# A fused attention and spectral-mixing kernel: the last 64 tokens laid out by batch halves, one of their two slots moved to ninth place, and 18 repeated matmuls added

## Chip, cores, metric

The kernel runs on one core of a Trainium2 chip. The metric is the device time of one execution in microseconds (us). Three runs of the kernel before gave 425.57, 425.76 and 425.96 us; the median, 425.76 us, is the time before.

## What is computed

Sliding-window causal attention (window 64) over 8 batches, 8 heads, 576 tokens and 64 channels a head; its result, as x of shape [8, 576, 512], goes through a spectral mixing layer with 64 modes.

```python
scores = scale * np.matmul(q, k.transpose(0, 1, 3, 2))      # masked to 0 <= rel < 64, then softmax
x = attn_out.transpose(0, 2, 1, 3).reshape(B, S, H * D)     # [8, 576, 512]
X = np.fft.rfft(x, axis=1)                                  # the first 64 modes are used
Yr = np.einsum('bmd,mde->bme', Xr, w_r) - np.einsum('bmd,mde->bme', Xi, w_i)
Yi = np.einsum('bmd,mde->bme', Xr, w_i) + np.einsum('bmd,mde->bme', Xi, w_r)
y = np.fft.irfft(Y, n=S, axis=1)
u = x + y
return u + np.maximum(u @ w_ch, 0.0)                        # float32, [8, 576, 512]
```

The two weight tensors `w_r` and `w_i` are 64 matrices of 512 x 512 in float32 each; all but the imaginary part of mode 0 are read, 127 matrices of 1 MB.

## The kernel before

**Attention, to about 142 us.** Windows of 512 query columns are worked off in a fixed order; the result is kept in SBUF as `x_sb` in bfloat16. A forward transform of the 64 modes by matmuls fills `XQ`.

**The weight stream, to about 390 us.** GpSimd's queue loads the 127 matrices, cast to bfloat16 on the way, one by one (`load_w`, L138) or two at a time (`load_two`, L144), into a ring of SBUF places. `half(i)` (L610) is the product of matrix i with `XQ`: 16 matmuls with 16 columns into one of two PSUM banks, `psys`. The banks change after 8 modes; at the change the finished one is copied to `YT` or `YTl`. `issue(i)` loads ahead as ring places come free, so a load waits on PE for the matmuls that read the place last. Other work is laid between the halves by a table of steps: from i = 33 the channel product of x (`channel_turn`, `channel`, into `Z0`), in 20 steps (`tables`) the tables of the inverse transform, `trigI` and `trigL`, and then the inverse transform of the first 48 modes (`add_z`, `make_u`, `last_tile`). Where little other work lies between two halves late in the stream, `fill(i)` (L895) repeats a matmul with 512 columns whose result is not used (`idle`, L900, PE row L902).

**The end.** The output has 36 pieces of 128 rows and 512 columns, 256 KB each. They are grouped in 18 slots of two pieces (index j). Slot s < 16 holds rows 128t to 128t + 127 of two batches (p, t = s // 4, s % 4). Slots 16 and 17 hold the last 64 tokens of four batches each: slot 16 of batches 0 to 3, slot 17 of batches 4 to 7. A piece of them is the last tokens of two batches. Before, the rows of such a piece are interleaved: partition 2i + k holds token 512 + i of the pair's batch k. `turns_bf`, a permuted identity, brings x into this order, and the columns of `trigI`, `trigL` and of the copy in `channel_turn` are interleaved in the same way.

The order of the slots is written out by hand: `seq` (L944), where `TURN` marks the place at which the late modes of batches 4 to 7 are turned (`turn_product`, `turn_rows`). For each slot PE lays the finished part of Z into a bank (`lay`, L955) and adds the late modes (`late_rows`, L962); ACT takes the positive part (`rectify`, L980); PE adds the late modes of the second term; DVE adds the kept u (`final`, L985), and SP stores the result. All stores go out on SP's queue in this order. The first two slots and the last one are stored piece by piece (L988), the others by one transfer of 512 KB for both pieces, whose pattern counts 128 partitions outermost (L991). Slots 16 and 17 take two transfers each: `out_of` gives, for each k, every second partition, 64 of them, with both pieces inside.

Of the kernel before, what the change touches and what calls it, by code (L numbers as in the profile page):

```python
# [10 lines left out]
FP32R = mybir.dt.float32r  # L11
# [9 lines left out]
def view(ap, off, dims):  # L21

    return bass.AP(ap.tensor, ap.offset + off, [list(ap.ap[0])] + [list(d) for d in dims])
# [3 lines left out]
def kernel(  # L27
# [17 lines left out]
    NT = 5  # L45
# [35 lines left out]
    def x_rows(b, t, n=128):  # L81
        return x_sb[:n, b // 2, (b % 2) * NT + block(b, t), :]
# [440 lines left out]
    YTl = late.tile([128, NC, B, R], FP32R, name="YTl")  # L523
    wlow = p2.enter_context(tc.tile_pool(name="wlow", bufs=1, side="right", reuse_waits="tile"))
    late2 = p2.enter_context(tc.tile_pool(name="late2", bufs=1, side="right", reuse_waits="tile"))
    trigI = late2.tile([128, S + 66], FP32R, name="trigI")
    trigL = late2.tile([128, S + 64], FP32R, name="trigL")

    py = ExitStack()
    turns_bf = late2.tile([128, 64, 2], BF16, name="turns_bf")  # L530

    ps_y = py.enter_context(tc.tile_pool(name="ps_y", bufs=1, space=PSUM, side="right", reuse_waits="tile"))
    psys = [ps_y.tile([128, DM], FP32, name=f"psy{i}") for i in range(2)]
# [113 lines left out]
    def inverse_tables():  # L647

        c = claim("tables", FP32)
        tmpi = Parts(c[0])  # L650
        pcol = tmpi.tile([128, 1], FP32, name="pcol")
        nc.gpsimd.iota(pcol, pattern=[[0, 1]], base=0, channel_multiplier=1,
                       allow_small_or_imprecise_dtypes=True)

        SW = S // 4
        pos = tmpi.tile([128, SW], FP32, name="pos")
        nc.gpsimd.iota(pos, pattern=[[1, SW]], base=0, channel_multiplier=0,
                       allow_small_or_imprecise_dtypes=True)
        nc.vector.tensor_copy(out=turns_bf, in_=view(ident_bf, 0, [[1, 64], [64, 2]]))

        def col(name):
            return tmpi.tile([128, 1], FP32, name=name)

        def floor(d, p, name):
            f = col(name)
            nc.vector.tensor_scalar(out=f, in0=p, scalar1=1.0 / d, scalar2=0.5 / d - 0.5,
                                    op0=ALU.mult, op1=ALU.add)
            nc.vector.tensor_scalar(out=f, in0=f, scalar1=MAGIC, scalar2=-MAGIC,
                                    op0=ALU.add, op1=ALU.add)
            return f  # L670

        f32 = floor(32, pcol, "f32")
        f64 = floor(64, pcol, "f64")
        lcol, odd, even = col("lcol"), col("odd"), col("even")
        nc.vector.scalar_tensor_tensor(out=lcol, in0=f32, scalar=-32.0, in1=pcol,
                                       op0=ALU.mult, op1=ALU.add)
        nc.vector.tensor_single_scalar(out=lcol, in_=lcol, scalar=float(E0), op=ALU.add)
        nc.vector.scalar_tensor_tensor(out=odd, in0=f64, scalar=-2.0, in1=f32,
                                       op0=ALU.mult, op1=ALU.add)
        nc.vector.tensor_scalar(out=even, in0=odd, scalar1=-1.0, scalar2=1.0,  # L680
                                op0=ALU.mult, op1=ALU.add)
        for tab, row in ((trigI, pcol), (trigL, lcol)):
            yield
            fa, fb = floor(2 * MG, row, "fa"), floor(MG, row, "fb")

            gcol, mcol = col("gcol"), col("mcol")
            nc.vector.scalar_tensor_tensor(out=gcol, in0=fa, scalar=-2.0, in1=fb,
                                           op0=ALU.mult, op1=ALU.add)
            nc.vector.tensor_tensor(out=mcol, in0=fa, in1=fb, op=ALU.subtract)
            nc.vector.scalar_tensor_tensor(out=mcol, in0=mcol, scalar=float(MG), in1=row,  # L690
                                           op0=ALU.mult, op1=ALU.add)
            coef, coefs, coefc = col("coef"), col("coefs"), col("coefc")
            nc.vector.tensor_single_scalar(out=coef, in_=mcol, scalar=0.0, op=ALU.is_equal)
            nc.vector.tensor_scalar(out=coef, in0=coef, scalar1=-1.0 / S, scalar2=2.0 / S,
                                    op0=ALU.mult, op1=ALU.add)
            nc.vector.tensor_tensor(out=coefs, in0=gcol, in1=coef, op=ALU.mult)
            nc.vector.tensor_tensor(out=coefc, in0=coef, in1=coefs, op=ALU.subtract)
            for i in range(4):
                yield
                mt2 = tmpi.tile([128, 2, SW], FP32, name="mti")  # L700
                mt = mt2[:, 0, :]
                nc.vector.tensor_scalar(out=mt, in0=pos, scalar1=float(i * SW), scalar2=mcol,
                                        op0=ALU.add, op1=ALU.mult)
                tis = tmpi.tile([128, SW], FP32, name="tis")
                gen_trig(tmpi, mt2, SW, mt, tis, "i")
                yield
                nc.vector.tensor_scalar(out=tis, in0=tis, scalar1=coefs, scalar2=None, op0=ALU.mult)
                o2 = 513 if tab is trigI else 512
                for c0, c1, o, k in ((0, SW, i * SW, 1),) if i < 3 else ((0, 80, 432, 1), (80, SW, o2, 2)):
                    nc.vector.scalar_tensor_tensor(  # L710
                        out=view(tab, o, [[k, c1 - c0]]), in0=mt[:, c0:c1], scalar=coefc,
                        in1=tis[:, c0:c1], op0=ALU.mult, op1=ALU.add)
        yield
        nc.vector.tensor_scalar(out=view(trigI, 512, [[2, 65]]), in0=trigI[:, 0:65], scalar1=0.0,
                                scalar2=None, op0=ALU.mult)
        last = [view(trigL, 512 + k, [[2, 64]]) for k in range(2)]
        nc.vector.tensor_scalar(out=last[1], in0=last[0], scalar1=odd, scalar2=None, op0=ALU.mult)
        nc.vector.tensor_scalar(out=last[0], in0=last[0], scalar1=even, scalar2=None, op0=ALU.mult)
        give(c)
# [24 lines left out]
    def channel_turn(s):  # L744
        pst = ps_t.tile([128, 2, NC, 128], BF16, name="pxt")
        for j, (b, t) in enumerate(slot_tiles(s)):
            for c in range(NC):
                nc.tensor.transpose(out=pst[:, j, c, :], in_=x_rows(b, t)[:, 128 * c:128 * c + 128],  # L748
                                    identity=ident_bf)
        o, i = xts[s % 2][0], pst.rearrange("p j c n -> p j (c n)")  # L750
        if s >= 4 * NP:
            o, i = (view(a, 0, [[128, 2 * NC]] + d) for a, d in ((o, [[1, 2], [2, 64]]), (i, [[64, 2], [1, 64]])))
        nc.vector.tensor_copy(out=o, in_=i)  # L753

    def channel(s, j):
        if j == 0:
# [37 lines left out]

    def first_rows(ps, b, t, k, x):

        parts = [(b, 128 * t)] if t < NT - 1 else [(b, 513), (b + 1, 512)]
        for n, (bb, o) in enumerate(parts):
            last = n == len(parts) - 1
            nc.tensor.matmul(out=ps, lhsT=trigI[:E0, o:o + 128], rhs=Yp[bb][0][:E0, k, :],  # L800
                             start=n == 0, stop=last and not x)
        if x:
            perm = ident_bf if t < NT - 1 else view(turns_bf, 0, [[1, 128]])
            nc.tensor.matmul(out=ps, lhsT=perm, rhs=x_rows(b, t), start=False, stop=True)

    def add_z(p, t):
        ps = ps_e.tile([128, 2, DM], FP32, name="pse", tag="pse")
# [80 lines left out]
    def out_of(s):  # L888
        if s < 4 * NP:
            p, t = divmod(s, 4)  # L890
            return [(slice(0, 128), out[2 * p:2 * p + 2, 128 * t:128 * t + 128, :])]
        b = 4 * (s - 4 * NP)
        return [(slice(k, 128, 2), out[b + k:b + k + 3:2, 512:576, :]) for k in range(2)]

    def fill(i):  # L895

        if i < T_I - 3 and i in thin:
            idle(psys[1 - mode_of(i) // MG % 2], LEAST - streamed[i])

    def idle(o, n):  # L900
        for _ in range(n):
            nc.tensor.matmul(out=o, lhsT=ident_bf, rhs=view(trigF, 0, [[1, DM]]), start=True, stop=True)  # L902

    with tc.manual_schedule(engines=ALL_FOUR):
# [36 lines left out]


        TURN = -1
        seq = [0, 4, 5, 1, 2, 6, 7, 3, TURN, 8, 12, 9, 13, 10, 16, 17, 14, 11, 15]  # L944
        NQ, TQ = len(seq), seq.index(TURN)
        assert sorted(seq) == list(range(-1, NS))

# [34 lines left out]
        def final(q, js=range(2)):  # L982
            u = U[seq[q]]
            for j in js:
                nc.vector.tensor_tensor(out=u[:, j, :], in0=bank(q, j), in1=u[:, j, :], op=ALU.add)  # L985
                if q in (0, 1, NQ - 1):
                    for pp, o in out_of(seq[q]):
                        nc.sync.dma_start(out=o[j], in_=u[pp, j, :])  # L988
                elif j:
                    for pp, o in out_of(seq[q]):  # L990
                        nc.sync.dma_start(out=o.rearrange("b p e -> p b e"), in_=u[pp])  # L991

        def pool(name, stack=p2, **kw):
            return stack.enter_context(tc.tile_pool(name=name, bufs=1, space=PSUM, reuse_waits="tile", **kw))
# [92 lines left out]
```

## Time and profile before

| What | Value |
|---|---|
| time before, median of 3 | 425.76 us |
| the profiled execution's own time | 425.57 us |
| its span, first to last instruction | 423.8 us |
| mean granted TensorE clock | 0.85 |
| PE matmul busy | 347.9 us, 82% |
| DVE, ACT, POOL busy | 188.8, 159.8, 81.7 us |
| DMA: queue of GpSimd (q0), queue of SP (q1) | 81.21 MB, 10.62 MB |
| HBM read, written | 162.53 MB, 9.44 MB |

Between two numbers divided by a bar, the first is the busy time of a group and the second the mean of one instruction. The span starts at the first instruction; places in it are given in us from there. Shares of busy time are means over the whole span; the stages named above are read one by one.

### The profile page before, as it was taken

To read this page: it belongs to the slowest core of one execution; us is meant where nothing else is said; L and a number is where in the kernel's file an instruction comes from. 1 tells how busy PE (TensorE), PEld (TensorE's weight loads), DVE (VectorE), ACT (ScalarE), POOL (GpSimd) and SP (SyncE) were. 2 spreads that over 40 slices of the span, in tenths; PEclk is the share of its full clock that TensorE was granted. 3 is DMA by queue.
4 is the path that set the end of the run, shared out by engine and by line. 5 is a ranking of instruction groups with operands and counts; after the bars stand their busy time and mean duration, and the time that the engine had idled before them with its cause. 6 is when DMAs were issued, how large, how long until landed. Compare 5 with 4: busy or idle time off the path is not lost.

```text
span 423.8 us, 11431 instructions
## 1 busy us (share of the span) xinstructions
PE 347.9 (82%) x5167; PEld 230.8 (54%) x5167; DVE 188.8 (45%) x359; ACT 159.8 (38%) x267; POOL 81.7 (19%) x146
## 2 busy tenths in 40 slices
PE   7899999999998775957659576667699999898994
PEld 3466666656654575735546455445465565554541
DVE  5576766676764101634341361211104344350885
ACT  5666865766864100212102110200023343330873
POOL 6231222231121230412111111210121112200000
PEclk9999999999999555866665766868579999999997
DMA  8999999999999999999999999999999999995598
GB/s 212 212 214 212 213 214 213 212 213 212 215 213 215 212 216 261 215 213 215 214 213 215 213 216 214 213 215 213 215 214 215 213 213 212 213 214 106 201 381 311
DMA packets 29920, 92.55 MB, mean 218 GB/s; under 512 B 2352, under 2 KB 2352, under 8 KB 29872
## 3 DMA queue, kind: packets, MB, share of 16 engines
q0 software_dynamic: 24624, 81.21, 95.9%
q1 hardware_dynamic: 5248, 10.62, 6.8%
q8 instruction: 40, 0.66, 0.6%
q14 instruction: 8, 0.07, 0.0%
HBM read 162.53 MB, written 9.44 MB: 406 GB/s over the span
## 4 chain that ended last, share of the span: by engine, by line
DMA 41%; PE 39%; DVE 7%; issue 6%; ACT 2%; POOL 0%; DVEq 0%; POOLq 0%; ACTq 0%
DMA wms<-in_moe_w_i_dram 22%; DMA wms<-in_moe_w_r_dram 15%; PE psy L618 6%; PE pso L343 6%; PE pst L247 5%; DMA wls<-in_moe_w_i_dram 5%; PE psv L264 3%; PE psx L365 3%; PE pss L962 2%; DVE x_sb L351 2%; PE pss L300 2%; PE pss L955 2%; PE pss L319 2%; PE psz L759 2%; DVE vT L59 2%
## 5 line engine op out<-in xcount | busy, mean ns | idle before, releaser
L759 PE MATMUL psz<-wch,xT 128*128 128x512 f32 x144 | 63.6, 583 | 0.0
L753 DVE CAST xT<-pxt 128x1024 fp32r<-128x1024 bf16 x18 | 22.0, 1225 | 81.2 <-PE pxt L748 81.0
L762 ACT CAST Z<-psz 128x1024 fp32r<-128x1024 f32 x18 | 18.2, 1012 | 104.2 <-PE psz L759 94.8
L325 ACT ACTIVATE et<-pss 128x512 bf16<-128x512 f32 x72 | 39.2, 600 | 13.7 <-PE pss L319 13.7
L618 PE MATMUL psy<-XQ,wms 128*128 128x16 bf16 x624 | 25.1, 192 | 20.2 <-DMA wms<-in_moe_w_i_dram 14.2
L618 PE MATMUL psy<-XQ,wls 128*128 128x16 bf16 x560 | 21.8, 192 | 23.6 <-DMA wls<-in_moe_w_r_dram 13.7
L759 PEld LDWEIGHTS psz<-wch,xT 128*128 128x128 f32 x144 | 36.6, 281 | 5.9
L618 PEld LDWEIGHTS <-wms 128*128 128x128 bf16 x624 | 21.3, 103 | 32.9 <-DMA wms<-in_moe_w_i_dram 17.6
L618 PEld LDWEIGHTS <-wls 128*128 128x128 bf16 x560 | 19.1, 105 | 33.4 <-DMA wls<-in_moe_w_r_dram 17.1
L343 PE MATMUL pso<-vt,et 128*64 128x65 bf16 (+1 forms) x576 | 32.3, 203 | 3.5 <-DVE x_sb L351 1.8
L811 DVE TENSOR_TENSOR Z<-pse,Z 128x1024 fp32r<-128x1024 f32 x16 | 19.6, 1224 | 29.5 <-PE pse L800 29.5
L343 PEld LDWEIGHTS <-et 128*64 128x64 bf16 (+1 forms) x576 | 22.2, 108 | 14.2 <-issue 6.7
L351 DVE TENSOR_TENSOR x_sb<-pso,rcp 128x640 bf16<-128x640 f32 x32 | 26.3, 822 | 0.9
L618 PE MATMUL psy<-XQ,wt 128*128 128x16 bf16 x560 | 20.5, 192 | 5.5 <-DMA wt<-in_moe_w_i_dram 3.0
L618 PEld LDWEIGHTS <-wt 128*128 128x128 bf16 x560 | 18.4, 104 | 11.3 <-DMA wt<-in_moe_w_i_dram 4.9
L59 DVE COPY vT<-pst 128x768 bf16<-128x768 bf16 x16 | 15.3, 958 | 12.9 <-PE pst L247 11.4
L980 ACT ACTIVATE pss<-pss 128x512 f32<-128x512 f32 x35 | 18.5, 581 | 4.9 <-PE pss L962 4.3
L59 DVE CAST YT<-psy 128x256 fp32r<-128x256 f32 x6 | 2.5, 423 | 38.7 <-PE psy L618 38.7
L748 PE MATMUL pxt<-ident_bf,x_sb 128*128 128x128 bf16 x144 | 15.1, 266 | 2.1 <-issue 2.1
L264 PE MATMUL psv<-ident_bf,vT 128*128 128x128 bf16 (+1 forms) x160 | 15.7, 226 | 0.9 <-DVE vT L59 0.6
L300 PE MATMUL pss<-band,ident_bf 64*64 64x512 bf16 x120 | 16.3, 396 | 0.0
L58 ACT COPY vt<-psv 128x768 bf16<-128x768 bf16 x16 | 12.9, 807 | 8.5 <-PE psv L264 8.4
(191 smaller groups left out, 599.1 us busy)
## 6 DMA issues: line engine op xcount, KB each, us to landing
wt<-in_moe_w_i_dram POOLq DMA_DIRECT2D x19, 512.0 KB, 20.0
wt<-in_moe_w_r_dram POOLq DMA_DIRECT2D x16, 512.0 KB, 19.0
wls<-in_moe_w_r_dram POOLq DMA_DIRECT2D x8, 1024.0 KB, 21.6
wms<-in_moe_w_i_dram POOLq DMA_DIRECT2D x7, 1024.0 KB, 22.0
wms<-in_moe_w_r_dram POOLq DMA_DIRECT2D x7, 1024.0 KB, 21.8
wls<-in_moe_w_i_dram POOLq DMA_DIRECT2D x6, 1024.0 KB, 21.2
rq<-in_q_dram POOLq DMA_DIRECT2D x8, 576.0 KB, 15.3
rv<-in_v_dram POOLq DMA_DIRECT2D x8, 576.0 KB, 13.4
```

The costliest lines, as they stand in the source:

```text
L59: return nc.vector.tensor_copy(out=o, in_=i)
L247: nc.tensor.transpose(out=ps[64 * hh:64 * hh + 64, c, :], in_=src[:, hh, (c0 + c) * D:(c0 + c + 1) * D], identity=ident_bf)
L264: nc.tensor.transpose(out=ps[r0:r0 + n, i, :], in_=vT[:, g, t0:t0 + n], identity=ident_bf)
L300: nc.tensor.matmul(out=pss[(2 * w + hh) % 3][64 * half:64 * half + 64, :], lhsT=ident_bf[pp, pp], rhs=view(band[pp], 128 * half, [[0, WIN ...
L325: nc.scalar.activation(out=et[:, hh, :], in_=pss[(2 * w + hh) % 3], func=ACT_F.Exp, scale=EX_SCALE)
L343: nc.tensor.matmul(out=pso[po, hh, block(b, i // 2) * VW:block(b, i // 2) * VW + D + 1], lhsT=et[pk, hh, col:col + 64], rhs=vt[pk, 1 - f % ...
L351: nc.vector.tensor_tensor(out=view(x_sb, b * NT * DM + g * D, [[4 * D, 2], [DM, NT], [1, D]]), in0=view(pso, 0, [[512, 2], [VW, NT], [1, D]]),
L618: nc.tensor.matmul(out=view(psy, off + 2 * B * e, [[1, 2 * B]]), lhsT=w[:, c, 128 * e:128 * e + 128], rhs=XQ[:, m // HM, c, :, 1 - im:3 - ...
L753: nc.vector.tensor_copy(out=o, in_=i)
L759: nc.tensor.matmul(out=psz[s][:, j, :], lhsT=xts[s % 2][0][:, j, 128 * c:128 * c + 128], rhs=wch[:, c, :], start=(c == 0), stop=(c == NC - 1))
L811: nc.vector.tensor_tensor(out=z, in0=ps, in1=z, op=ALU.add)
L980: nc.scalar.activation(out=bank(q, j), in_=bank(q, j), func=ACT_F.Relu)
```

## The change

- A piece of slots 16 and 17 holds the first of its two batches on partitions 0 to 63 and the second on 64 to 127. `turns_bf` and its copy go, and the strided writes into `trigI`, `trigL` and `xT` become plain ones.
- A piece of slots 16 and 17 is stored as soon as its own add is done, by one transfer from 128 partitions to `out[b:b + 2, 512:576, :]`, instead of two transfers from 64 partitions each after both adds.
- Slot 16 moves from the 15th place to the ninth, ahead of `TURN`; slot 17 moves from the 16th to the 12th place of the slots.
- `fill` adds one repeated matmul after each of the halves 20 to 37.

```diff
-    trigI = late2.tile([128, S + 66], FP32R, name="trigI")
+    trigI = late2.tile([128, S + 128], FP32R, name="trigI")
...
-    turns_bf = late2.tile([128, 64, 2], BF16, name="turns_bf")
...
-        nc.vector.tensor_copy(out=turns_bf, in_=view(ident_bf, 0, [[1, 64], [64, 2]]))
...
-                o2 = 513 if tab is trigI else 512
-                for c0, c1, o, k in ((0, SW, i * SW, 1),) if i < 3 else ((0, 80, 432, 1), (80, SW, o2, 2)):
+                o2 = 576 if tab is trigI else 512
+                for c0, c1, o in ((0, SW, i * SW),) if i < 3 else ((0, 80, 432), (80, SW, o2)):
...
-        nc.vector.tensor_scalar(out=view(trigI, 512, [[2, 65]]), in0=trigI[:, 0:65], scalar1=0.0,
-                                scalar2=None, op0=ALU.mult)
-        last = [view(trigL, 512 + k, [[2, 64]]) for k in range(2)]
+        nc.vector.tensor_scalar(out=view(trigI, 512, [[128, 2], [1, 64]]), in0=view(trigI, 0, [[64, 2], [1, 64]]),
+                                scalar1=0.0, scalar2=None, op0=ALU.mult)
+        last = [trigL[:, 512 + 64 * k:576 + 64 * k] for k in range(2)]
...
-        o, i = xts[s % 2][0], pst.rearrange("p j c n -> p j (c n)")
-        if s >= 4 * NP:
-            o, i = (view(a, 0, [[128, 2 * NC]] + d) for a, d in ((o, [[1, 2], [2, 64]]), (i, [[64, 2], [1, 64]])))
-        nc.vector.tensor_copy(out=o, in_=i)
+        nc.vector.tensor_copy(out=xts[s % 2][0], in_=pst.rearrange("p j c n -> p j (c n)"))
...
-        parts = [(b, 128 * t)] if t < NT - 1 else [(b, 513), (b + 1, 512)]
+        parts = [(b, 128 * t)] if t < NT - 1 else [(b, 576), (b + 1, 512)]
...
-            perm = ident_bf if t < NT - 1 else view(turns_bf, 0, [[1, 128]])
-            nc.tensor.matmul(out=ps, lhsT=perm, rhs=x_rows(b, t), start=False, stop=True)
+            nc.tensor.matmul(out=ps, lhsT=ident_bf, rhs=x_rows(b, t), start=False, stop=True)
...
-            return [(slice(0, 128), out[2 * p:2 * p + 2, 128 * t:128 * t + 128, :])]
+            return out[2 * p:2 * p + 2, 128 * t:128 * t + 128, :]
         b = 4 * (s - 4 * NP)
-        return [(slice(k, 128, 2), out[b + k:b + k + 3:2, 512:576, :]) for k in range(2)]
+        return [out[b + 2 * j:b + 2 * j + 2, 512:576, :] for j in range(2)]
 
     def fill(i):
 
-        if i < T_I - 3 and i in thin:
-            idle(psys[1 - mode_of(i) // MG % 2], LEAST - streamed[i])
+        n = LEAST - streamed[i] if i in thin else i in range(20, 38)
+        if i < T_I - 3:
+            idle(psys[1 - mode_of(i) // MG % 2], n)
...
-        seq = [0, 4, 5, 1, 2, 6, 7, 3, TURN, 8, 12, 9, 13, 10, 16, 17, 14, 11, 15]
+        seq = [0, 4, 5, 1, 2, 6, 7, 3, 16, TURN, 8, 12, 9, 17, 13, 10, 14, 11, 15]
...
-                if q in (0, 1, NQ - 1):
-                    for pp, o in out_of(seq[q]):
-                        nc.sync.dma_start(out=o[j], in_=u[pp, j, :])
+                if q in (0, 1, NQ - 1) or seq[q] >= 4 * NP:
+                    nc.sync.dma_start(out=out_of(seq[q])[j], in_=u[:, j, :])
                 elif j:
-                    for pp, o in out_of(seq[q]):
-                        nc.sync.dma_start(out=o.rearrange("b p e -> p b e"), in_=u[pp])
+                    nc.sync.dma_start(out=out_of(seq[q]).rearrange("b p e -> p b e"), in_=u)
```

More of the change, by code (lines that the diff above doesn't have):

```diff
@@ L707, in inverse_tables @@
                 nc.vector.tensor_scalar(out=tis, in0=tis, scalar1=coefs, scalar2=None, op0=ALU.mult)
-                o2 = 513 if tab is trigI else 512
-                for c0, c1, o, k in ((0, SW, i * SW, 1),) if i < 3 else ((0, 80, 432, 1), (80, SW, o2, 2)):
+                o2 = 576 if tab is trigI else 512
+                for c0, c1, o in ((0, SW, i * SW),) if i < 3 else ((0, 80, 432), (80, SW, o2)):
                     nc.vector.scalar_tensor_tensor(
-                        out=view(tab, o, [[k, c1 - c0]]), in0=mt[:, c0:c1], scalar=coefc,
+                        out=tab[:, o:o + c1 - c0], in0=mt[:, c0:c1], scalar=coefc,
                         in1=tis[:, c0:c1], op0=ALU.mult, op1=ALU.add)
         yield
-        nc.vector.tensor_scalar(out=view(trigI, 512, [[2, 65]]), in0=trigI[:, 0:65], scalar1=0.0,
-                                scalar2=None, op0=ALU.mult)
-        last = [view(trigL, 512 + k, [[2, 64]]) for k in range(2)]
+        nc.vector.tensor_scalar(out=view(trigI, 512, [[128, 2], [1, 64]]), in0=view(trigI, 0, [[64, 2], [1, 64]]),
+                                scalar1=0.0, scalar2=None, op0=ALU.mult)
+        last = [trigL[:, 512 + 64 * k:576 + 64 * k] for k in range(2)]
         nc.vector.tensor_scalar(out=last[1], in0=last[0], scalar1=odd, scalar2=None, op0=ALU.mult)
```

## Prediction

> **What bounds the kernel now.** I read the page's slices and queues first, then the waits, then the end in windows, then the DMA view of the last 12 us.
>
> ```profile
> DMA  8999999999999999999999999999999999995598
> GB/s 212 212 214 212 213 214 213 212 213 212 215 213 215 212 216 261 215 213 215 214 213 215 213 216 214 213 215 213 215 214 215 213 213 212 213 214 106 201 381 311
> DMA packets 29920, 92.55 MB, mean 218 GB/s; under 512 B 2352, under 2 KB 2352, under 8 KB 29872
> ...
> q1 hardware_dynamic: 5248, 10.62, 6.8%
> q8 instruction: 40, 0.66, 0.6%
> ```
>
> The 16 DMA engines are full at some 213 GB/s until 384 us: the weight stream sets the time there. Then a second stage begins, the stores.
>
> ```profile
> POOL wls L144 <- PE psy L618: 70.6, 14, 13.0
> ...
> PEld L618 <- DMA wms<-in_moe_w_i_dram: 17.6, 10, 3.9
> ```
>
> GpSimd waits for PE to free a ring place (total us, times, longest), PE waits for weights; since the engines never run dry, neither costs time.
>
> ```profile
> 400.00:414.00 14.00, 14.00 (x64) 6.71 (x63) 12.79 (x21) 10.03 (x20) 0.00 (x0) 1.00 1.03 381
> 414.00:416.00 2.00, 2.00 (x10) 0.90 (x8) 1.77 (x4) 1.54 (x4) 0.00 (x0) 1.00 0.76 288
> 416.00:422.00 6.00, 1.98 (x7) 0.73 (x6) 3.15 (x6) 1.51 (x3) 0.00 (x0) 0.78 1.02 379
> 422.00:423.00 1.00, 0.00 (x0) 0.00 (x0) 0.00 (x0) 0.00 (x0) 0.00 (x0) 0.50 0.37 141
> ```
>
> The last two columns are the DMA share and GB/s. From 400 us the stores run at 381 GB/s with all engines full, except in 414 to 416; DVE's last add ends at 419.15, yet data moves until 422.54. So the stores set the end, although PE is full until 418.
>
> ```profile
> DMA  9999999998049999999999999999999999500000
> GB/s 403 382 403 403 341 355 410 389 389 321 14 177 396 362 410 355 335 403 369 369 376 382 389 348 396 369 396 389 389 362 369 430 355 403 212 0 0 0 0 0
> ```
>
> This is 412 to 424 in 0.3 us slices: one hole, at 415.0 to 415.4, in front of slot 16's first store.
>
> ```profile
> 412.63 5.73 SPq L991 DMA_DIRECT2D out_dram<-x_sb  x7
> 418.62 1.75 SPq L988 DMA_DIRECT2D out_dram<-x_sb  x2
> ```
>
> **What the stores are spread over.** SP's queue q1 shows 5248 packets. The output is 9.44 MB in rows of 2 KB, 4608 packets; the one load (1152 KB in pieces of 4608 B) has 256. The other 384 are 24 transfers times 16: every transfer ends with 16 small packets, one an engine. So each store of before runs on all 16 engines, 8 packets an engine for a 256 KB piece. All have the same outermost count on both sides: 128 and 128, or 64 and 64 for slots 16 and 17.
>
> **The four new transfers.** Source: 128 partitions. Destination: 2 batches outermost, 64 rows inside. It is the only transfer of the kernel whose sides differ in their outermost count, and the trace of before has no row for it. Its bounds: spread over 16 engines as every row shows, or cut at the only outermost division that both sides share, in two, so that two engines do it. I take the second: each engine of every row before gets one start and one count along the outermost dimension of both sides, and here only two equal parts can be given in that way. The 16-engine rows all have counts that 16 divides, so they don't speak against it. The Trainium skill states this as a rule ("DMA: Bandwidth & Descriptors", section "Why a DMA increments its semaphore by 16 and not by 1"): the number of engines is the largest up to 16 that divides the slowest count of both sides, and on SP's kind of queue the lowest-numbered engines are used. By that rule it is 2, the same two for all four; the trace's 16 small packets at 128 and at 64 agree, and no run here shows a 2 yet.
>
> Price. Crowded, an engine moves 381/16 = 23.8 GB/s, a 2 KB packet in 86 ns. Alone it is hardly faster: at 398.7 to 398.96, when one engine has work left, its packets start 80 ns apart. A narrow piece is 64 packets on each of two engines, 5.1 us, against 0.69 us over 16.
>
> The sum, for the two engines:
> - Slot 16's first piece. DVE's adds run back to back at 0.61 us from 399.73 to 403.99; two more end at 405.2, so it is issued at about 405.3. Until then 16 of 36 pieces are issued; the packets in the trace show 11.7 landed, so 4.3 x 8 = 34 packets wait on each engine.
> - The rest: 4 x 64 = 256 packets of the narrow pieces, and 16 ordinary pieces with 8 each, 128.
> - 34 + 256 + 128 = 418 packets at 80.4 ns (16 in 1.286 us on an engine that catches up in this stage) = 33.6 us, to 438.9. All other stores are issued by then: compute ends at about 419, and SP reuses a completion count after eight transfers, so slot 10 waits for slot 16's first piece (413.2 by the same count), 14 for the second (418.3), 11 and 15 for slots 8, 12 and 9 (by 422.2). Each comes before the two engines run dry. The queue behind these waits on SP is stores alone, and nobody but the end waits for those.
> - From the last packet to the end of the span is 1.25 us (422.54 to 423.79), outside the span 1.77 (425.57 - 423.8). Total 438.9 + 1.25 + 1.77 = 441.9, against 425.57: +16.3. On the median, which lies 0.2 higher, 442.1.
>
> The Trainium skill's page "DMA: Bandwidth & Descriptors" ("Specifications") gives an engine about 27 GiB/s, 71 ns for a packet; with it the sum, an estimate, would be 437.8. The trace's 80 ns are for this very packet and decide.
>
> Bounds: every packet at the crowded 86 ns, +2.3 (444.4). Below, the step from 86 to 80 once more, 74 ns, -2.7 (439.4), and 0.5 to 1 for where the stage starts.
>
> **Slot order and hole.** Slot 16's pace moves ahead of TURN (1.2 us a slot there by SP's issues from 398.68 to 403.47, against 1.4 to 1.6 behind it) and the hole at 415 goes: up to -0.6. With two engines behind by 16 us this is covered; it counts in the rival below.
>
> **18 repeated matmuls.** The row L902 in the timeline has 6 in 1.46 us at full clock, 0.24 each; at clock 0.5, granted from 139.5 to 173.6, twice that: 4.4 to 8.8 us on PE between about 156 and 178. What hides it: the loads in flight. The issue at 169.37 waited 13.0 us for PE, but the load issued before it, at 155.78, landed at 179.87, so PE may be 10.5 us later before the engines run dry. Taken: 0. If the cover were gone it would cost what exceeds 10.5 us. The first clocked-up windows may come earlier, which PE then waits out for weights (0). 36 more instructions of 64 B (0.66 MB for 10,334) are a seventh of one of q8's 40 packets, each 0.95 us on one engine: 0 to 1.0, taken 0 since the fetches run ahead and the last one lies past the stream.
>
> **The rest.** The copy for `turns_bf` goes, two of 18 `xT` copies (1225 ns each, row L753) and three table writes lose their strides: all on DVE between 165 and 310 us, where it is a third busy. 0 both ways. The permuted identity and the plain one cost the same (391 ns, rows L804).
>
> **Rivals.**
> 1. *The new pieces spread over 16 engines.* For: every row of before does. Then the stores are as before without the hole: the backlog at the issues behind TURN, 1.07 us at the smallest that made none (412.63), grows by some 0.2 through the faster slot ahead of TURN. 425.76 - 0.6 = 425.1; with the short hole at 398.7 closed too (0.3, if the instruction fetch at 397.1 on one engine made the fourth issue take 1.04 us), 424.8. It decides from 16 engines; at 8 a piece is 16 packets on each, 32 more in all, and the end would already be 2 us late (2.6 less the 0.6). Not slower; chance 0.14.
> 2. *Narrow stores hold up SP.* If the issue itself waits until its 64 packets an engine are taken, the next store starts only then, 0.85 us after (issue at 395.71 to first packet at 396.56). For: SP's issues take 0.6 to 1.14 us late in the stage, against 0.37. Against: those are 64-row or crowded ones, still far below 5 us. Four such pauses, 3.4 us on the two engines: 445.5. Chance 0.14.
> 3. *The matmuls starve the weight stream.* Beyond 10.5 us of delay each further us counts once. 8.8 is the most, so I give it 0.02; at 2 us too many it would be 444.
>
> **Numbers.** Plain two engines 0.70 (442.1), SP held up 0.14 (445.5), sixteen 0.14 (425.1), starved 0.02. Range 438.5 to 447: the first two cases with their bounds, and little else. A measurement of this kernel can tell 0.2%, 0.85 us, from no change. Slower 0.86; of the 0.14, 424.91 is the line: same 0.10, faster 0.04.
>
> **What would show it.** Right: q1 has 5248 - 4 x 14 = 5192 packets, as narrow transfers end with 2 small ones; from about 423 to 439 the DMA share is near 2/16 at some 50 GB/s, with every compute engine idle; 256 KB stores land 8 to 20 us after issue; the stream still ends near 389.7. Wrong: 5248 packets, a last packet at 422, stores landing in 2.5 us. A DMA share below 1 between 165 and 200 would speak for the third rival; SP issues of 5 us for the second.

## The result and the profile after

The kernel after takes 444.05 us (median of 5 runs, 443.97 to 444.32), the kernel before 425.96 us beside it on the same chip: 1.0428 times as long, 95% interval 1.0416 to 1.0440. The forecast was 442.1, in a range from 438.5 to 447.0. The profiled execution took 444.17 us with a span of 442.4 us; before, 425.57 and 423.8.

The page of the kernel after, slices, packets and SP's queue:

```profile
DMA  8999999999999999999999999999999999928443
GB/s 209 211 213 214 211 213 213 213 213 214 214 213 214 213 254 220 214 215 214 214 213 214 214 215 214 214 214 214 213 214 214 212 206 214 195 74 329 170 163 140
DMA packets 29864, 92.55 MB, mean 209 GB/s; under 512 B 2296, under 2 KB 2296, under 8 KB 29816
...
q1 hardware_dynamic: 5192, 10.62, 6.6%
```

The weight stream is as before, full at some 213 GB/s. The last slices are new: 329, 170, 163 and 140 GB/s where before ended with 381 and 311. q1 has the forecast 5192 packets, and the 56 that are missing are all among those under 512 B (2352 before, 2296 now): each of the four new transfers ends with 2 small packets instead of 16, so two engines carry it. The completion counts in the trace agree: an ordinary store adds 16 as it lands, one an engine, and slot 16's first piece adds two, at 415.71 and 415.82. The rule of the Trainium skill's page "DMA: Bandwidth & Descriptors" (section "Why a DMA increments its semaphore by 16 and not by 1"), the largest number up to 16 that divides the slowest count of both sides, gives 2 for counts of 128 and 2; the trace agrees.

The end of the kernel after in windows (length; busy time of PE, its weight load, DVE, ACT, POOL; granted clock; DMA share; GB/s):

```profile
396.60:408.00 11.40, 11.40 (x57) 5.67 (x56) 11.10 (x19) 8.80 (x17) 0.00 (x0) 1.00 0.99 368
408.00:410.40 2.40, 2.40 (x12) 1.10 (x8) 2.03 (x4) 2.09 (x4) 0.00 (x0) 1.00 0.12 11
410.40:413.00 2.60, 2.60 (x13) 1.28 (x12) 2.22 (x5) 1.57 (x4) 0.00 (x0) 1.00 0.12 47
413.00:417.50 4.50, 4.25 (x19) 1.83 (x17) 4.28 (x8) 3.75 (x8) 0.00 (x0) 1.00 0.98 350
417.50:427.00 9.50, 0.78 (x2) 0.18 (x1) 1.58 (x3) 0.10 (x1) 0.00 (x0) 0.52 0.14 54
427.00:434.50 7.50, 0.00 (x0) 0.00 (x0) 0.00 (x0) 0.00 (x0) 0.00 (x0) 0.50 0.98 355
434.50:441.00 6.50, 0.00 (x0) 0.00 (x0) 0.00 (x0) 0.00 (x0) 0.00 (x0) 0.50 0.14 54
```

Three stretches have a share of 0.12 to 0.14, two engines of 16, at some 50 GB/s. Between them all engines work for a while, and then only the two again. PE, DVE and ACT have next to nothing left from 419 on. Where the first narrow piece starts, from 408.0 to 410.4, even the two engines hardly move anything: 11 GB/s. The last packet ends at 441.16 (422.54 before).

SP's own timeline in the same stretch (start, time its issues took, line, transfer, count):

```profile
405.68 1.99 SPq L982 DMA_DIRECT2D out_dram<-x_sb  x2
408.22 4.37 SPq L984 DMA_DIRECT2D out_dram<-wms  x1
...
415.10 6.70 SPq L982 DMA_DIRECT2D out_dram<-x_sb  x2
421.97 4.84 SPq L984 DMA_DIRECT2D out_dram<-wms  x1
426.91 3.68 SPq L984 DMA_DIRECT2D out_dram<-x_sb  x3
```

An issue took 0.37 us in most of before, as here:

```profile
406.82 0.37 SPq L991 DMA_DIRECT2D out_dram<-wms  x1
```

In the kernel after, three single ones took 4.37, 6.06 (the second of the two at 415.10) and 4.84 us, 5.09 in the mean, each with narrow pieces queued ahead of it. A narrow piece of 64 packets at 80.4 ns keeps its engine busy for 5.15 us. That SP waits there for room on the two engines is my reading; the trace shows only the length.

### The profile page after: what moved, and what is told of

Same layout as the page of the kernel before. It is cut to its first block, busy times and chain, and to the rows that moved or that the text cites. A ratio compares the mean times of both kernels' runs of the same rounds, so it can differ in the third digit from the quotient of the medians.

```text
span 442.4 us, 11438 instructions
## 1 busy us (share of the span) xinstructions
PE 350.8 (79%) x5156; PEld 233.0 (53%) x5185; DVE 188.6 (43%) x358; ACT 160.0 (36%) x267; POOL 81.8 (18%) x146
## 2 busy tenths in 40 slices
DMA packets 29864, 92.55 MB, mean 209 GB/s; under 512 B 2296, under 2 KB 2296, under 8 KB 29816
## 3 DMA queue, kind: packets, MB, share of 16 engines
q1 hardware_dynamic: 5192, 10.62, 6.6%
## 4 chain that ended last, share of the span: by engine, by line
PE 41%; DMA 39%; DVE 6%; issue 4%; ACT 3%; POOL 1%; DVEq 0%; POOLq 0%; ACTq 0%
DMA wls<-in_moe_w_r_dram 20%; DMA wls<-in_moe_w_i_dram 14%; PE pso L343 6%; PE pst L247 5%; PE psy L617 4%; DMA wms<-in_moe_w_i_dram 3%; PE psv L264 3%; DMA wms<-in_moe_w_r_dram 3%; PE pss L957 2%; PE pss L950 2%; PE pss L300 2%; DVE x_sb L351 2%; PE psx L365 2%; PE pss L319 2%; PE psf L795 2%
## 5 line engine op out<-in xcount | busy, mean ns | idle before, releaser
L754 PE MATMUL psz<-wch,xT 128*128 128x512 f32 x144 | 59.9, 554 | 0.0
L754 PEld LDWEIGHTS psz<-wch,xT 128*128 128x128 f32 x144 | 34.3, 264 | 5.3
L746 PE MATMUL pxt<-ident_bf,x_sb 128*128 128x128 bf16 x144 | 16.3, 284 | 0.0
```

The costliest lines, as they stand in the source:

```text
L754: nc.tensor.matmul(out=psz[s][:, j, :], lhsT=xts[s % 2][0][:, j, 128 * c:128 * c + 128], rhs=wch[:, c, :], start=(c == 0), stop=(c == NC - 1))
```

## Experiments

Theory: the two engines that do the narrow pieces set the end. Rivals: SP's held issues set it; the new order of the slots or the repeated matmuls cost something of their own. A second question is the 2.3 us from 408.0 to 410.4, which the forecast did not have.

### 1. The narrow transfers taken away: e1_halves

The kernel after, each piece of slots 16 and 17 by two transfers of 64 partitions:

```diff
-                if q in (0, 1, NQ - 1) or seq[q] >= 4 * NP:
+                if seq[q] >= 4 * NP:
+                    for k in range(2):
+                        nc.sync.dma_start(out=out_of(seq[q])[j][k], in_=u[64 * k:64 * k + 64, j, :])
+                elif q in (0, 1, NQ - 1):
```

> The changed kernel, but each piece of slots 16 and 17 goes out in two transfers of 64 partitions to 64 rows, so both sides count 64 outermost. Theory (two engines carry a transfer whose outermost counts are 128 and 2): all stores run on 16 engines again, the hole in front of slot 16 is gone, 425.1 to 425.5 us; 5184 data and small packets plus 4 x 16 for four more transfers, 5312 packets on SP's queue. Rival (the order of the slots, the batch halves or the repeated matmuls cost the time): stays near 444 us.

Measured: 426.97 us, 1.0025 times the time before (1.0016 to 1.0033), q1 5312 packets. 17 of the 18 us are gone with this edit alone. The rest, about 1 us over the time before, I had not expected. Windows of this kernel:

```profile
400.00:408.00 8.00, 8.00 (x39) 4.00 (x39) 7.70 (x14) 5.89 (x11) 0.00 (x0) 1.00 1.01 378
408.00:412.00 4.00, 4.00 (x19) 1.94 (x18) 3.27 (x6) 2.89 (x6) 0.00 (x0) 1.00 0.95 301
412.00:416.00 4.00, 4.00 (x20) 1.88 (x18) 3.79 (x7) 2.95 (x6) 0.00 (x0) 1.00 0.99 342
```

The engines are nearly full in all three, but while the stores from one half of the partitions are under way they move 301 and 342 GB/s instead of 378. A packet takes 102 and 94 ns there in the mean, a tenth of them 121 ns and more, in place of 88. The kernel before also stores 64 partitions at a time, every second one, and holds 379 to 381 GB/s wherever it is not in its hole. So the number of partitions alone is not it. At least two differences remain that no run here takes apart: which partitions they are, and transfers half as large (128 KB, 4 packets an engine, in place of 256 KB and 8). The Trainium skill's page "SBUF — State Buffer" ("Door 1: The DMA port swizzle") has partitions 0 to 63 on half of the DMA ports; the slower packets would fit that, but no run here shows a port.

### 2. One slot narrow: e5_one

The kernel after, slot 16 as there, slot 17 by halves as in e1_halves:

```diff
-                if q in (0, 1, NQ - 1) or seq[q] >= 4 * NP:
+                if seq[q] == 4 * NP + 1:
+                    for k in range(2):
+                        nc.sync.dma_start(out=out_of(seq[q])[j][k], in_=u[64 * k:64 * k + 64, j, :])
+                elif q in (0, 1, NQ - 1) or seq[q] == 4 * NP:
```

> The kernel after, with slot 16 still stored by narrow transfers (two engines) and slot 17 by two transfers of 64 partitions for each piece. Theory (the two engines' count of packets sets the end): from the start of the first narrow piece, seen at 410.4 in the kernel after, the two engines have 2 x 64 + 18 x 8 = 272 packets left instead of 384, 112 x 80.4 ns = 9.0 us fewer: last packet 432.2, time 435.1; q1 shows 5248 - 28 + 32 = 5252 packets; the pause of 2.3 us stays, since it belongs to the first narrow piece. Rival (the end is set by SP's held issues): the two issues held 6.06 and 4.84 us behind slot 17 are gone, 10.9 us less: 433.1. Rival (a narrow transfer costs a fixed sum once, whatever their number): 444.

Measured: 435.69 us, ratio 1.0232 (1.0218 to 1.0246), q1 5252 packets, last packet 432.52. That is 0.6 from the count of packets and 2.6 from the rival with SP's held issues; the fixed sum is far off. Each narrow piece costs the two engines 64 packets where an ordinary one costs 8. The count gives 9.0 us for the two pieces that are gone; from first to last packet of the stores it is 35.54 us here and 44.54 in the kernel after, 9.0 less. (The medians differ by 8.4; this profiled run's stores begin 0.36 us later.) Two of its windows:

```profile
408.40:410.70 2.30, 2.30 (x12) 1.10 (x8) 1.92 (x4) 2.03 (x4) 0.00 (x0) 1.00 0.12 11
...
430.20:432.60 2.40, 0.00 (x0) 0.00 (x0) 0.00 (x0) 0.00 (x0) 0.00 (x0) 0.50 0.12 48
```

The pause is there again, and the end is again two engines alone.

### 3. One transfer from 128 partitions, over 16 engines: e3_both

The kernel before with the new order, and each piece stored by one transfer as soon as its add is done. The rows stay interleaved, so the destination counts 64 rows outermost with 2 batches inside. No repeated matmuls:

```diff
-        return [(slice(k, 128, 2), out[b + k:b + k + 3:2, 512:576, :]) for k in range(2)]
+        return [(slice(0, 128), [out[b + 2 * j:b + 2 * j + 2, 512:576, :].rearrange("k i e -> i k e") for j in range(2)])]
...
-        seq = [0, 4, 5, 1, 2, 6, 7, 3, TURN, 8, 12, 9, 13, 10, 16, 17, 14, 11, 15]
+        seq = [0, 4, 5, 1, 2, 6, 7, 3, 16, TURN, 8, 12, 9, 17, 13, 10, 14, 11, 15]
...
-                if q in (0, 1, NQ - 1):
+                if q in (0, 1, NQ - 1) or seq[q] >= 4 * NP:
```

> The kernel before with its interleaved rows, the new order of the slots, and each piece of slots 16 and 17 stored by one transfer from 128 partitions whose destination is read as 64 rows outermost and 2 batches inside; no repeated matmuls. If the number of engines is the largest up to 16 that divides both outermost counts (64 and 128), it is 16: 425.1 us, 5248 packets on SP's queue, no hole at 415. If unequal counts on the two sides are what narrows a transfer, it stays narrow: some 440 us or more.

Measured: 425.87 us, ratio 0.9998 (0.9989 to 1.0007), q1 5248 packets: 16 engines with unequal counts, 128 against 64. One transfer, the early issue and the order are therefore harmless; the destination's 2 outermost batches are what makes a transfer narrow. The time is 0.8 us above what I had expected. The hole at 415 is gone, yet the time is that of before, since from 398 to 399 the stage now moves 125 GB/s (before: 238):

```profile
398.00:399.00 1.00, 1.00 (x7) 0.42 (x6) 1.00 (x3) 0.88 (x3) 0.00 (x0) 1.00 0.39 125
...
408.00:416.00 8.00, 8.00 (x37) 3.82 (x36) 7.02 (x12) 5.76 (x12) 0.00 (x0) 1.00 1.02 378
```

### 4. The order: e4_late and e7_order

The kernel after with the old order, and the kernel before with the new one (the `seq` lines above, one way and the other).

> The changed kernel with the order of before: both last-token slots 14th and 15th behind the turn. Theory (the two engines' packets set the end): four narrow pieces and six ordinary ones are left when slot 10's store has landed at 415.1, 256 + 48 packets at 80.4 ns, 24.4 us, so the last lands near 439.5 and the time is 442.5; with a pause of 2.3 us as at 408 in the changed kernel, 444.8. So the order is worth less than 1 us either way. Rival (the early place makes the other stores wait behind the narrow ones on SP, and that costs): 430 us or less when they come late.

> The kernel before with the new order of the slots alone; the rows stay interleaved, stored by two transfers of 64 partitions after both adds. Theory (the order closes the hole at 415 and opens another place of waiting ahead of it): 425.2 to 425.9, q1 5248 packets. Rival (the order itself costs, hidden in the kernel after by the narrow stores): over 426.7.

Measured: 444.61 us, ratio 1.0442 (1.0428 to 1.0456), for the first, and 425.87 us, ratio 0.9998 (0.9989 to 1.0007), for the second. The order is worth 0.6 us on the kernel after by the medians, with intervals that overlap, and nothing that can be told on the kernel before. In e4_late the pause comes with the first narrow piece again, now at 415.6:

```profile
415.60:417.50 1.90, 1.90 (x10) 0.76 (x7) 1.90 (x4) 1.44 (x3) 0.00 (x0) 1.00 0.13 14
```

e7_order shows where the gain of the closed hole is lost again. Two of its windows, then one of the kernel before:

```profile
398.00:400.60 2.60, 2.60 (x13) 1.13 (x12) 2.60 (x5) 2.36 (x6) 0.00 (x0) 1.00 0.59 211
...
408.00:416.00 8.00, 8.00 (x37) 3.83 (x36) 7.04 (x12) 5.81 (x11) 0.00 (x0) 1.00 1.03 379
```

```profile
408.00:416.00 8.00, 8.00 (x36) 3.63 (x33) 7.19 (x12) 6.10 (x13) 0.00 (x0) 1.00 0.96 359
```

From 408 to 416 no hole is left, but at 398 to 400.6 the engines are only 0.59 busy. In the trace a fetch of instructions (queue q8), one packet of 16 KB on one engine, starts at 396.86 and takes 1.72 us, in the middle of the first stores. That q8 serves PE is inferred, from its 0.66 MB for PE's 10,334 instructions and from experiment 5.

### 5. The repeated matmuls: e2_repeat

The kernel before with the new `fill`:

```diff
-        if i < T_I - 3 and i in thin:
-            idle(psys[1 - mode_of(i) // MG % 2], LEAST - streamed[i])
+        n = LEAST - streamed[i] if i in thin else i in range(20, 38)
+        if i < T_I - 3:
+            idle(psys[1 - mode_of(i) // MG % 2], n)
```

> The kernel before with the 18 repeated matmuls alone. Theory: 425.8 us, within 0.2% of before; PE reaches the load issue of 169.4 us about 1 us later, the DMA engines stay full. Rival (they starve the stream or move the clock): 427 us or more, or a gain by a clock granted earlier, 425 or less.

Measured: 425.77 us, ratio 0.9998 (0.9990 to 1.0007): the matmuls cost nothing that can be told. They move the fetch from 397.11 to 392.62, ahead of the stores. In the first 4 us of its stores the stage then loses 0.30 us against a steady 381 GB/s, in place of 0.53, but the hole at 415 is a little longer instead (e2_repeat, then before):

```profile
412.00:416.00 4.00, 4.00 (x19) 1.88 (x18) 3.64 (x7) 2.75 (x7) 0.00 (x0) 1.00 0.89 329
```

```profile
412.00:416.00 4.00, 4.00 (x19) 1.85 (x18) 3.62 (x7) 2.78 (x6) 0.00 (x0) 1.00 0.90 337
```

That fits a stage that waits there for compute and so gains nothing from an earlier start; a difference of 8 GB/s over 4 us is little to go by.

### 6. All three harmless parts together: e8_three and e11_again

The edits of e3_both and e2_repeat in one kernel, run twice:

> The kernel before with the new order, each piece of slots 16 and 17 stored by one transfer over 16 engines once its add is done (rows still interleaved), and the 18 repeated matmuls. Alone, the first two closed the hole at 415 but lost about as much at 398, where a fetch of PE's instructions at 396.9 held up an issue; the matmuls alone moved that fetch to 392.6, ahead of the stores. Theory (the two losses are what both single runs kept): neither hole is left, last packet 422.2, time 425.1 to 425.3. Rival (the fetch doesn't hold up the issue, the stage starts late for another reason): 425.8, with the idle time at 398 still there.

> The same kernel as e8_three once more, beside fresh runs of the kernel before, since one of its eleven times, 429.65, lay 4 us above all others and made its interval too wide to tell. If the two closed holes are worth 0.5 us: median 425.2 to 425.5 and an interval wholly below 1. If they are worth nothing: 425.8 and an interval around 1.

Measured: 425.42 us, ratio 0.9998 (0.9979 to 1.0016), and in the second run 425.32 us against 425.85, ratio 0.9988 (0.9979 to 0.9997). Two windows of e8_three:

```profile
398.00:399.00 1.00, 1.00 (x10) 0.39 (x6) 1.00 (x2) 0.88 (x3) 0.00 (x0) 1.00 1.01 389
...
408.00:416.00 8.00, 8.00 (x39) 3.83 (x35) 7.08 (x12) 6.25 (x12) 0.00 (x0) 1.00 1.01 376
```

With the fetch at 392.86, neither stretch has a hole. From first to last packet of the stores it is 25.47 us, against 25.98 before. This kernel is the fastest of all: some 0.5 us under the kernel before by the medians of both runs, though only the second run's interval lies below 1, so the gain is at the edge of what can be told. The three kernels whose fetch starts at 396.9 to 397.1 (before, e3_both, e7_order) lose 0.5 to 1.2 us against a steady 381 GB/s in the first 4 us of their stores. All others (e10_gap aside, whose stores begin with the extra piece) fetch at 392.4 to 393.0 and lose 0.3 us. But these are also the ones with the repeated matmuls, so that the fetch itself makes the loss is likely and not shown.

### 7. The same pieces from GpSimd's queue: e6_pool

```diff
-                if q in (0, 1, NQ - 1) or seq[q] >= 4 * NP:
+                if seq[q] >= 4 * NP:
+                    nc.gpsimd.dma_start(out=out_of(seq[q])[j], in_=u[:, j, :])
+                elif q in (0, 1, NQ - 1):
```

> The kernel after, with the four narrow transfers issued from GpSimd's queue instead of SP's. Theory: still two engines for each, but whether the same two for all four isn't known for this queue. If the pairs differ, no engine has more than 64 narrow packets besides its 34 waiting and 128 ordinary ones: 226 x 80.4 ns = 18.2 us from 405.3, last packet 423.5, time 426.5, and 428.8 if the pause of 2.3 us comes as well. If they are the same two, 444. If this queue cuts the piece for 16 engines, 425.5. SP's issues are held less than 2 us in every case but the second.

Measured: 436.44 us, ratio 1.0246 (1.0232 to 1.0260), which none of my cases gave. The page's line of GpSimd's queue, and two windows:

```profile
q0 software_dynamic: 26736, 82.27, 94.7%
```

```profile
410.40:416.00 5.60, 5.60 (x25) 2.64 (x26) 5.02 (x9) 3.97 (x8) 1.58 (x2) 1.00 0.89 232
...
430.00:433.00 3.00, 0.00 (x0) 0.00 (x0) 0.00 (x0) 0.00 (x0) 0.00 (x0) 0.50 0.13 49
```

q0 has 2112 packets more than in the other kernels: for each transfer 64 data packets of 4 KB, 448 of 8 bytes and 16 that end it. While they run, the engines are 0.89 busy at 232 GB/s, and the 2 KB packets of SP's queue take 100 to 158 ns, by the mean of each microsecond from 410 to 424, instead of 87. Toward the end the engines fall idle one after another (shares of 0.62, 0.47, 0.24 and 0.07 in the windows from 428 on) instead of fourteen at once, so the pieces were on more than two of them. Which engines, and how much of the loss is the 8-byte packets, stays open. SP's issues were held up to 2.68 us, more than the 2 us that I had allowed for. The one at 408.60 took 0.37 us, and yet little moved from 408.4 to 410.4; the packets of that stretch are 4 KB and 8-byte ones, so this says little about the slow start of the kernel after.

### 8. The pause: e9_early and e10_gap

The kernel after with one more narrow store, to a place that the real one overwrites later; in e9_early in the middle of the weight stream, in e10_gap between stream and stores:

```diff
             nc.scalar.copy(out=last_u(p), in_=ps[:, 0, :])
+            if p == 0:
+                nc.sync.dma_start(out=out[0:2, 512:576, :], in_=last_u(p))
```

```diff
         nc.vector.tensor_copy(out=YY[0][:, 1, :], in_=psys[0])
+        nc.sync.dma_start(out=out[0:2, 512:576, :], in_=view(YTl, 0, [[1, DM]]).bitcast(FP32))
```

> The kernel after, with one more narrow store of 256 KB in the middle of the weight stream (the kept u of the first pair of batches, to the place that slot 16's first piece later overwrites). It asks whose the pause of 2.3 us is that stood in front of the first narrow piece. If it is the kernel's first transfer of this form that pauses: the extra store takes it, and at 408 the two engines go straight on at 80 ns a packet; from the landing of the last ordinary packet to the last packet of all 2.3 us less than the 33.1 of the kernel after (408.0 to 441.16), so 30.8. If every narrow transfer pauses that meets two empty engines: slow packets and the pause are there again, 33.1. The time is 444.05 plus what the weight stream loses to 64 more packets on two engines, 0 to 5.1 us, and 2.3 less in the first case. q1 5192 + 128 + 2 = 5322 packets.

> The kernel after, with one more narrow store of 256 KB in the gap between the weight stream and the first stores (part of YTl, to the same place, overwritten later), issued at about 392, when no other packet moves. If a narrow transfer pauses whenever it starts on empty engines, its first packets take 0.3 to 1 us each and it ends at about 392.9 + 2.3 + 5.1 = 400.3; if the pause at 408 came from what surrounded it there (the end of the ordinary stores), it ends at 398. In the first case the two engines are 3.8 us behind when the stores of the stage start and don't run empty at 408, so no pause there: 444.05 + 3.8 - 2.3 = 445.5. In the second 444.05 + 1.5 - 2.3 or, with the pause at 408 again, + 1.5: 443.3 to 445.5, told apart by the packets.

Measured: 444.94 us, ratio 1.0445 (1.0427 to 1.0462), and 445.64 us, ratio 1.0461 (1.0445 to 1.0477). One window of e9_early, then two of e10_gap:

```profile
408.40:410.80 2.40, 2.40 (x12) 1.10 (x8) 2.02 (x4) 2.08 (x4) 0.00 (x0) 1.00 0.11 11
```

```profile
393.30:396.10 2.80, 2.72 (x19) 1.34 (x16) 1.81 (x3) 2.17 (x5) 0.00 (x0) 1.00 0.13 31
...
410.30:412.20 1.90, 1.90 (x9) 0.84 (x8) 1.37 (x4) 1.31 (x4) 0.00 (x0) 1.00 0.11 17
```

In e9_early the pause is unchanged. From where the other 14 engines have ended their ordinary packets (408.03 in the kernel after, 408.49 here) to the last packet of all it is 33.0 us, against 33.1. So it is not the price of the first transfer of this form. In e10_gap the extra store starts slowly too, with no store ahead of it: its first 20 packets on each engine take 2.7 us in place of 1.6, some of them 200 to 406 ns long. SP issued nothing from 392.8 to 396.4, so a held issue is not needed for slow packets. But the second half of my expectation failed: the two engines ran into slot 16's first piece without having run empty, and the slow packets came there again, 306 to 549 ns each. So engines that run empty are not needed for it. The time is as forecast by accident, the longer lag of the two engines and the pause adding up to about what I had put down for the lag alone. Slot 17's pieces, queued while the two engines still had a long way to go, show a few packets of 200 to 350 ns and no stretch in which the two engines stand. What makes the start slow stays open.

The trace of the kernel after shows that the slow packets are not the narrow piece's alone. The ordinary store ahead of it, issued at 405.04, sends its last small packet only at 410.36 and lands at 410.69, 15 of its 16 engines having ended by 408.11. So one of the two engines still has ordinary packets when the pause begins, and its first 64 narrow ones then run at 80 ns each, from 410.36 to 415.48. In e4_late, e5_one, e9_early and e10_gap, too, the 16th small packet of the store ahead comes 0.9 to 2.2 us after the 15th, inside the slow stretch.

## Why the forecast was right

**Two engines.** Right: 5192 packets, the two engines alone at some 50 GB/s, and e1_halves takes 17 us away by widening these four transfers alone. e3_both shows the rule from its other side: unequal counts of 128 and 64 still give 16 engines. The reason that the prediction gives, one start and one count for each engine, no run shows: the traces tell how many engines and packets, not which rows an engine takes. Its packets 80 ns apart at 398.7 come from two engines, not one; the price is the same. The sign of a stretch from 423 to 439 with two engines alone came only in part: from 427 to 434.5 all 16 work, on stores that SP had held back.

The time by itself would not have told this case from rival 2: 444.05 lies 1.95 above the one's 442.1 and 1.45 below the other's 445.5. The trace and e5_one tell them apart.

**The sum.** 34 waiting packets from 405.3 end at 408.03. In the trace 14 engines end theirs by 408.03, though by two small errors that cancel (the issue came at 405.68, with 28 waiting); on the engine that ends last of all it is 410.3. From there the sum holds: 384 packets at 80.4 ns are 30.9 us, the trace has 30.8, from 410.36 to 441.16. The tail is 1.24 us (1.25) and the part outside the span 1.77 (1.77). e5_one changed the number of packets and moved as the sum says (9.0 us).

**The term that was mis-sized.** The passage from the waiting packets to the first narrow piece. The sum let the one follow the other at once, 0 us; it cost 2.3 us, with seven packets of 276 to 1048 ns between 408.1 and 410.4. Some 0.5 us of it is that one engine was six ordinary packets behind the others at 408.03 (counted back from its 16th small packet, an estimate); the rest is the slow packets. From 404 to 416 us in slices of 0.3 us:

```profile
DMA  9999999999999412101101111111116999999999
GB/s 396 389 362 355 403 375 389 348 410 355 410 382 369 123 14 7 7 0 7 7 0 27 41 48 55 48 55 48 55 48 239 362 396 335 382 335 375 362 355 341
```

It is the whole difference: 441.9 + 2.3 is the profiled run's 444.2. The forecast of 442.1 is 1.9 short of 444.05, and its upper bound, every packet at 86 ns, gave 444.4 for a reason that did not occur.

**Rival 2, SP held up.** Half right. SP is held, longer than the rival had it (5.1 us in place of 0.85), the issues of 5 us that the prediction named as its sign are there, and this is why the other 14 engines stand idle from 408 to 413 and from 417.5 to 427. But the two engines always have work ahead, 25 packets in each microsecond in which they are alone from 411 to 441, as the sum had argued, so it costs nothing at the end. The pause is not this rival: it is one, not four, and e10_gap has slow packets at 393.8 to 395.4 while SP issues nothing.

**Rival 1, sixteen engines.** It did not happen. Its price of 425.1 was 0.8 too low for e3_both without the matmuls (425.87) and 0.2 to 0.3 too low with them (425.3 to 425.4). What it missed is that the two holes must go together; each edit alone left the one or the other. The short hole at 398 was put down to the instruction fetch, and the kernels with the fetch moved support that without proving it.

**Rival 3, the matmuls.** PE's busy time between 150 and 200 us rose by 4.7 us, within the forecast's 4.4 to 8.8 (before, then after):

```profile
150.00:200.00 50.00, 35.58 (x670) 29.25 (x666) 15.04 (x43) 7.42 (x12) 11.68 (x20) 0.63 1.07 224
```

```profile
150.00:200.00 50.00, 40.26 (x684) 31.26 (x686) 14.31 (x42) 7.43 (x12) 11.29 (x19) 0.60 1.07 224
```

GpSimd's queue in the kernel after:

```profile
155.10 1.11 POOL L138 DMA_DIRECT2D wt<-in_moe_w_i_dram  x2
170.34 0.71 POOL L144 DMA_DIRECT2D wls<-in_moe_w_r_dram  x1 [14.13 <-PE psy L617]
```

The issue that waited for PE came at 170.34 instead of 169.37, 1 us later. The cover was read wrongly: in the trace of before, the load issued at 155.78 lands engine by engine from 177.94 to 183.12, not at 179.87, so by this the first engines would have run dry after some 8.6 us of delay and not 10.5. Against 1 us that changes nothing. The DMA share from 150 to 200 is 1.07 in both kernels, and e2_repeat settles it.

**Order, hole and the rest.** Taken as covered, and so they are: e4_late differs by 0.6 us, within the two intervals. The stream ends as before (share 0.04 and 0.02 from 389 to 396.6).

## What to carry to other kernels

Look at the outermost count of both sides of a transfer before anything else: here one with 128 partitions on one side and 2 batches on the other ran on two engines, and one with 128 and 64 on 16. Price a narrow one by the packets that its few engines then have to move, not by its bytes. The small packets that end each transfer, 16 or 2, give the number of engines away in one line of the page. And when two short holes stand in one stage, close both before judging either: here each alone measured as nothing, together they gave some 0.5 us, at the edge of what could be told.

## What the hardware showed that I had not expected

- Where the first narrow store of the stage follows ordinary ones, both of its engines are slow: 2.3 us in the kernel after, 1.9 to 2.4 in e4_late, e5_one, e9_early and e10_gap, with packets of 0.2 to 1.0 us, the last ordinary ones of one engine among them. Then 80 ns each.
- Three of SP's issues behind narrow stores were held 4.4 to 6.1 us in the kernel after; one narrow piece keeps its engines busy for 5.15 us.
- With stores from partitions 0 to 63 and 64 to 127 in turn among the others (128 KB each) the engines moved 301 to 342 GB/s; with stores from every second partition (256 KB) or from all 128, 376 to 381 where no hole was.
- The same narrow piece from GpSimd's queue came as 4 KB packets of 159 ns when undisturbed, with seven 8-byte packets for each.
- One 16 KB fetch of instructions, 1.0 to 1.7 us on one engine, among the first stores goes with a loss of up to 1 us at the start of the stage.
